# Batch 0's first weight columns by row chunks, and two up blocks begun ahead of the products with v

## Chip, cores, metric

One core of one Trainium2 chip. The metric is the device time of one execution in microseconds (us); lower is better. Five engines run their own instruction streams side by side and wait for each other by semaphores: PE (matmuls, with PEld as its weight loads), DVE (element-wise work), ACT (activations and copies), POOL (GpSimd; here it issues the loads) and SP (it issues the stores). DMA queues move the data between DRAM and the on-chip memory.

## What is computed

Attention with keys and values projected along the sequence, then a layer that takes the larger of two products:

```python
k_proj = np.einsum('ks,bhsd->bhkd', E, k)          # 64 rows instead of 1024
v_proj = np.einsum('ks,bhsd->bhkd', F, v)
attn   = softmax(q @ k_proj.T / 8)                 # 8 batches, 8 heads, 1024 x 64
x      = attn @ v_proj                             # as 8192 tokens x 512
g      = np.maximum(x @ w1, x @ w2)                # 8192 x 1024
out    = g @ w_out                                 # 8192 x 512
```

The kernel uses max(a, b) = relu(a - b) + b: it forms wd = w1 - w2 once, computes relu(x @ wd), and adds x @ (w2 @ w_out), where m = w2 @ w_out is also formed once. Inputs are float32 in DRAM; the loads convert them to float16.

## The kernel before

**Tiling.** A batch has 1024 tokens. Attention is done in four parts: two groups of four heads (g = 0, 1) times two halves of the tokens (j = 0, 1). `xt` holds x transposed: four row chunks r of 128 features (chunk r = heads 2r and 2r+1), so part (g, j) writes row chunks 2g and 2g+1 for token half j. An *up block* (j, fb) is relu(x @ wd) for token half j and 128 columns fb of wd: four matmuls, one for each row chunk r of wd and xt, summed in one PSUM bank (line 481), then a relu on ACT (line 490; for fb = 3 on DVE, line 492). Batches 1 to 7 use a form with fewer multiplications (lines 702 and 794), which begins as soon as batch 0's up blocks, m and the sums are done.

**Order.** The kernel is scheduled by hand (`manual_schedule`): every engine runs its instructions in the order in which the program issues them, and an instruction that waits holds back everything behind it on its engine. Batch 0's attention is a written-out list (lines 911 to 960); all that follows is a list `slots` of small steps, worked through in order (lines 986 to 1020 and 1126 to 1132). If a step of that list returns a function, that function runs right after the next step.

**Loads.** POOL issues every load in program order (lines 102 to 137): batch 0's k, q and v, then w2 and w1 in column pieces, w_out, then batch 1's k, v, q and batch 2's k. A weight row is addressed as (g, p, z): row chunk r = 2g + z, partition p. The first 256 columns go as four loads, w2 and w1 for g = 0 and the same for g = 1, each with both z (128 KB in float16; lines 122 to 127). Columns 256 to 511 and the rest go as one load for each z (lines 128 to 136).

**Around the change.** `step_at(g, j)` multiplies the exponentials with v (32 x 256 matmuls, line 346) into two banks and then scales them into `xt` with two DVE multiplications, o = 0 and 1 (line 401); it has a hook `between` between those two. `step_kv(.., "v")` projects v (line 189) and copies it to `vp` (line 201). `step_wd(f0, r0, r1)` forms wd for columns from f0 and row chunks r0 to r1 on DVE (line 497). `step_w2t(f0)` transposes 256 columns of w2 on PE (line 513) and copies them with ACT (line 519); this feeds m. PSUM has four banks `mm0` to `mm3` taken in turn (`mm_bank`) and a pair of double banks `att`, also in turn (`att_banks`). The order of the end of the written list, before:

```python
    step_kv(t, 4, 8, "v", True, copy=nc.scalar.copy, between=lambda: step_dn(t, 1, 1))
    step_inv(t, 1, 1)
    att_banks()
    for f0 in (0, 128):
        step_wd(f0, 0, 2, 128)
    step_at(t, 1, 0, True)
    u0, u1 = [*up_slots(t, 0)], [*up_slots(t, 1)]
    step_wd(0, 2, 4)
    step_at(t, 1, 1, True)
    first_banks = turn[0:2], turn[2:4]
    for i in range(2):
        for u in u0, u1:
            u[i](r1=2)
    step_w2t(0, True)
```

So row chunks 0 and 1 of the up blocks (0,0), (1,0), (0,1), (1,1) come after all products with v. The slots then finish (0,0) and (0,1), transpose w2's next 256 columns, finish (1,0) and (1,1), form wd for columns 256 to 511 (`wd[1]`, line 497 with all four row chunks) and go on with up block (0,2).

Of the kernel before, what the change touches and what calls it, by code (L numbers as in the profile page):

```python
# [12 lines left out]
ALU = mybir.AluOpType  # L13
# [3 lines left out]
def kernel(  # L17
# [12 lines left out]
    nc = tc.nc  # L30
# [8 lines left out]
    NDC = DM // 128  # L39
# [17 lines left out]
    turn = [0, 1, 2, 3]  # L57

    def mm_bank(dtype=FP32, n=None):
        if n is None:  # L60
            n = turn.pop(0)
            turn.append(n)
        return ps.tile([128, 512 if dtype == FP32 else 1024], dtype, tag=f"mm{n}", name="mm_ps")

    def att_banks(dtype=FP32):
        return ps.tile(
            [128, 2, 512 if dtype == FP32 else 1024], dtype, tag="att", bufs=2, name="att_ps"
        )
# [4 lines left out]
    def big(n, dtype=FP16):  # L73
        return const.tile([128, 16384 // mybir.dt.size(dtype) // 2], dtype, tag=f"big{n}", name=f"big{n}")
# [19 lines left out]
    def alloc(t, n):  # L94
        t[n] = kvq.tile([128, H, NC, D], FP16, tag="kvq", name=f"{n}_sb")

    def load_all(t, b, n, src):
        alloc(t, n)
        load(t, n, src, b, 0, H)

    def load(t, n, src, b, h0, h1):
        nc.gpsimd.dma_start(  # L102
            out=t[n][:, h0:h1],
            in_=src[b, h0:h1].rearrange("h (p c) d -> p h c d", c=NC),
        )
# [13 lines left out]
    w1_sb = big(1).rearrange("p (r f) -> p r f", r=NDC)  # L119
    w2_sb = big(2).rearrange("p (r f) -> p r f", r=NDC)  # L120
    wo_sb = const.tile([128, NFB, DM], FP16, tag="wo", name="wo_sb")
    for g in range(2):
        for w_sb, w in ((w2_sb, moe_w2), (w1_sb, moe_w1)):
            nc.gpsimd.dma_start(
                out=w_sb.rearrange("p (g z) f -> p g z f", z=2)[:, g, :, 0:256],
                in_=w.rearrange("(g p z) f -> p g z f", p=128, z=2)[:, g, :, 0:256],
            )
    for w_sb, w, f0, f1 in (
        (w2_sb, moe_w2, 256, 512), (w1_sb, moe_w1, 256, 512), (w2_sb, moe_w2, 512, DF),
# [2 lines left out]
        for z in range(2):  # L132
            nc.gpsimd.dma_start(
                out=w_sb.rearrange("p (g z) f -> p g z f", z=2)[:, :, z, f0:f1],
                in_=w.rearrange("(g p z) f -> p g z f", p=128, z=2)[:, :, z, f0:f1],
# [220 lines left out]
    def values_into(t, g, j, at_ps):  # L356
        for z in range(2):
            tiles_into(
                lambda o: at_ps[o][:, z * W : (z + 1) * W], t["ex", g, j],
                lambda rows, hh: vp_of(t, 4 * g + hh, rows, z),  # L360
            )

    def new_xt(t):
        t["xt"] = xpool.tile([128, NP2, 2, HALF], FP16, tag="xt", name="xt_sb")

    def x_out(t, g, j):
        return t["xt"][:, 2 * g : 2 * g + 2, :, j * W : (j + 1) * W]
# [16 lines left out]
    def step_inv(t, g, j):  # L384
        ld = t["ld", g, j]
        nc.scalar.activation(out=ld, in_=ld, func=ACTF.Exp, scale=-1.0)

    def step_at(t, g, j, att=False, between=None):
        if "xt" not in t:
            new_xt(t)  # L390
        ld = t.pop(("ld", g, j))
        if att:
            both = att_banks()
            at_ps = [both[:, o, :] for o in range(2)]
        else:
            at_ps = [mm_bank() for _ in range(2)]
        values_into(t, g, j, at_ps)
        for o in range(2):
            if o and between is not None:
                between()  # L400
            nc.vector.tensor_tensor(
                out=x_out(t, g, j)[:, :, o, :],
                in0=at_ps[o].rearrange("q (z n) -> q z n", z=2),
                in1=ld[:, o, None, :].broadcast_to([128, 2, W]),
                op=ALU.mult,
            )
# [61 lines left out]
    wd_sb = const.tile([128, NDC, DF], FP16)  # L468
    m_sb = const.tile([128, NDC, DM], FP16)
    w2t_sb = big(3).rearrange("p (f m) -> p f m", f=NFB)  # L470


    def up_slots(t, j):
        t["gt", j] = gt = gpool.tile([128, NFB, HALF], FP16, tag="gt", name="gt_sb")
        for fb in range(NFB):
            def up(fb=fb, r0=0, r1=NDC):
                if r0 == 0:
                    t["up", j, fb] = mm_bank(n=None if r1 == NDC else first_banks[j][fb])
                h_ps = t["up", j, fb]
                for r in range(r0, r1):  # L480
                    nc.tensor.matmul(  # L481
                        out=h_ps,
                        lhsT=wd_sb[:, r, fb * 128 : (fb + 1) * 128],
                        rhs=t["xt"][:, r, :, j * W : (j + 1) * W],
                        start=(r == 0), stop=(r == NDC - 1),
                    )
                if r1 < NDC:
                    return
                if fb != 3:
                    nc.scalar.activation(out=gt[:, fb, :], in_=h_ps, func=ACTF.Relu)  # L490
                else:
                    nc.vector.tensor_scalar_max(gt[:, fb, :], h_ps, 0.0)
            yield up


    def step_wd(f0, r0=0, r1=NDC, n=256):
        nc.vector.tensor_tensor(
            out=wd_sb[:, r0:r1, f0 : f0 + n], in0=w1_sb[:, r0:r1, f0 : f0 + n],
            in1=w2_sb[:, r0:r1, f0 : f0 + n], op=ALU.subtract,
        )  # L500

    def step_wd_rows(f0):
# [6 lines left out]
    def step_w2t(f0, att=False):  # L509
        ps_t = att_banks(FP16)[:, 0, :] if att else mm_bank(FP16)  # L510
        for f in range(2):
            for r in range(NDC):
                nc.tensor.transpose(  # L513
                    out=ps_t[:, (f * NDC + r) * 128 : (f * NDC + r + 1) * 128],
                    in_=w2_sb[:, r, f0 + f * 128 : f0 + (f + 1) * 128],
                    identity=ident16,
                )
        fb = f0 // 128
        nc.scalar.copy(
            out=w2t_sb[:, fb : fb + 2, :].rearrange("q f m -> q (f m)"), in_=ps_t  # L520
        )

# [386 lines left out]
    t = tiles[0]  # L911
# [30 lines left out]
    step_dn(t, 1, 0)  # L942
    step_sc(t, 1, 1)
    step_at(t, 0, 0)
    step_at(t, 0, 1)
    step_inv(t, 1, 0)
    step_kv(t, 4, 8, "v", True, copy=nc.scalar.copy, between=lambda: step_dn(t, 1, 1))
    step_inv(t, 1, 1)
    att_banks()
    for f0 in (0, 128):  # L950
        step_wd(f0, 0, 2, 128)
    step_at(t, 1, 0, True)
    u0, u1 = [*up_slots(t, 0)], [*up_slots(t, 1)]
    step_wd(0, 2, 4)
    step_at(t, 1, 1, True)
    first_banks = turn[0:2], turn[2:4]
    for i in range(2):
        for u in u0, u1:
            u[i](r1=2)
    step_w2t(0, True)  # L960


    load_all(tiles[1], 1, "k", k)
    wt = [lambda f0=f0: step_w2t(f0) for f0 in range(0, DF, 256)]
    wd = [lambda f0=f0: step_wd(f0) for f0 in range(0, 512, 256)]
    wd += [lambda f0=f0: step_wd_rows(f0) for f0 in range(512, DF, 256)]
    f = lambda s, *a: lambda: s(tiles[0], *a)

    def loads(b, *names):
        for n in names:  # L970
            b_ = b + (n == "k" and b < 2)
            if (b_, n) == (1, "q"):
                alloc(tiles[1], "q")
                for c in (0, NC // 2):
                    nc.gpsimd.dma_start(
                        out=tiles[1]["q"][:, :, c : c + NC // 2],
                        in_=q[1].rearrange("h (p c) d -> p h c d", c=NC)[:, :, c : c + NC // 2],
                    )
            elif (b_, n) == (2, "q"):
                alloc(tiles[2], "q")  # L980
                for h in (0, H // 2):
                    load(tiles[2], "q", q, 2, h, h + H // 2)
            elif b_ < B:
                load_all(tiles[b_], b_, n, {"k": k, "v": v, "q": q}[n])

    slots = [
        (0, lambda: u0[0](r0=2)), (1, lambda: u0[1](r0=2)), (None, lambda: loads(1, "v", "q", "k")),
        (None, lambda: step_w2t(256, True)),
        (2, lambda: u1[0](r0=2)), (3, lambda: u1[1](r0=2)),
        (None, wd[1]), (4, u0[2]), (5, u0[3]),  # L990
# [46 lines left out]
    t = tiles[1]  # L1037
    at_slot((0, 22), new_attn, t)
    at_slot((0, 22), lambda: turn.__setitem__(slice(None), [2, 3]))
    for n, x in enumerate((  # L1040
# [4 lines left out]
        for name in x.split():  # L1045
# [6 lines left out]
            else:  # L1052
                g, j = int(name[2]), int(name[3])
# [13 lines left out]
    t = tiles[2]  # L1067
# [8 lines left out]
    for b in range(3, B):  # L1076
        t = tiles[b]
        n = 2 * b - 3
# [13 lines left out]
    for i, (new, old) in enumerate(zip([*groups[1:], none], groups)):  # L1092
        n, h = divmod(i + 2, 2)
# [9 lines left out]
    for n, (b, o) in enumerate(units):  # L1103
        u = U[b, o]
# [13 lines left out]
        if n:  # L1118
            end = ("U", n - 1, 1, 6) if n > 1 else ("P", 0, 6, 1)
            m = 0 if n == last else 2  # L1120
# [45 lines left out]
```

## Time and profile before

| | |
|---|---|
| median of 3 runs | 319.96 us (319.69, 319.96, 320.4) |
| the profiled execution | 319.73 us in all, of which the profile's span is 318.0 us |
| PE busy | 312.1 us, 98% of the span, 3920 matmuls |
| PEld, DVE, ACT, POOL busy | 253.5, 240.4, 206.1, 40.0 us |
| granted TensorE clock | 1.00 in every stretch |
| HBM read and written | 57.15 MB and 16.78 MB |

A row of the timeline gives the start, the length of a run of like instructions, the engine and line, the tiles written and read, the count, and in brackets the idle time of the engine just before and what ended it. Matmuls overlap: a matmul on 512 columns is shown as 379 ns long, but eight of them in a row take 1.90 us, one every 0.216 us. DVE and ACT instructions overlap a little as well: the scaling in line 401 is shown as 0.68 us and repeats every 0.60 us. The DMA view gives the time from the start of an issue to its landing.

### The profile page before, as it was taken

What the parts mean: (1) busy time and instruction counts of PE and PEld (TensorE: products, weight loads), DVE (VectorE), ACT (ScalarE), POOL (GpSimd) and SP (SyncE); (2) the same over time, 40 slices, a digit from 0 to 9 for tenths busy, and PEclk for the clock granted to TensorE, in tenths of its full rate; (3) what the DMA queues carried; (4) which work ended last, traced back from release to release, by engine and by line L of the source; (5) the groups of instructions that cost most, each with busy time, mean ns of one, the idle gap of its engine ahead of it and who ended that gap; (6) DMA issues with size and microseconds to landing.
All of it is one profiled execution on the core that took longest, in us unless ns stands there. A gap on an engine that the chain in (4) does not pass through costs nothing.

```text
span 318.0 us, 9177 instructions
## 1 busy us (share of the span) xinstructions
PE 312.1 (98%) x3920; PEld 253.5 (80%) x3920; DVE 240.4 (76%) x437; ACT 206.1 (65%) x372; POOL 40.0 (13%) x63
## 2 busy tenths in 40 slices
PE   8989999999999999999999999999999999999996
PEld 3555588788887888788887888788887888888885
DVE  2366888877969696996969696996969696969683
ACT  2476843777776777477776778477776777765541
POOL 8269002003000300030000400040000000000000
DMA  7999999999969899899989999989969131303124
GB/s 184 203 200 197 204 206 203 207 180 157 205 119 197 152 217 245 212 182 172 237 196 213 165 200 244 221 154 179 235 142 207 45 102 35 101 33 102 35 99 132
DMA packets 76424, 53.41 MB, mean 168 GB/s; under 512 B 29536, under 2 KB 76000, under 8 KB 76384
## 3 DMA queue, kind: packets, MB, share of 16 engines
q0 software_dynamic: 30688, 28.05, 56.4%
q1 hardware_dynamic: 45408, 24.58, 32.2%
q8 instruction: 30, 0.49, 0.6%
q10 hardware_dynamic: 288, 0.20, 0.2%
q14 instruction: 10, 0.08, 0.1%
HBM read 57.15 MB, written 16.78 MB: 233 GB/s over the span
## 4 chain that ended last, share of the span: by engine, by line
PE 92%; DMA 4%; POOL 1%; ACT 1%; DVE 0%; issue 0%; POOLq 0%; DVEq 0%
PE mm_ps L794 47%; PE mm_ps L702 27%; PE mm_ps L481 4%; DMA v_sb<-in_v_dram 4%; PE att_ps L346 3%; PE mm_ps L189 3%; PE mm_ps L334 2%; PE mm_ps L590 2%; PE att_ps L231 1%; PE mm_ps L305 1%; POOL k_sb L102 0%; POOL q_sb L102 0%; ACT ld_sb L382 0%; ACT ex_sb L374 0%; DVE o_sb L892 0%; PE att_ps L513 0%
## 5 line engine op out<-in xcount | busy, mean ns | idle before, releaser
L676 ACT COPY p_sb<-mm_ps 128x512 f32<-128x512 f32 x179 | 101.8, 592 | 49.4 <-PE mm_ps L702 27.6
L794 PEld LDWEIGHTS <-big 128*128 128x128 f16 x768 | 73.6, 98 | 11.8 <-issue 3.6
L794 PE MATMUL mm_ps<-T_sb,big 128*128 128x256 f16 x576 | 76.9, 273 | 0.0
L717 DVE TENSOR_TENSOR gt_sb<-mm_ps,p_sb 128x512 f16<-128x512 f32 x56 | 38.5, 688 | 43.9 <-PE mm_ps L702 43.6
L702 PE MATMUL mm_ps<-big,big 128*128 128x256 f16 x336 | 50.4, 273 | 0.0
L702 PEld LDWEIGHTS <-big 128*128 128x128 f16 x448 | 43.8, 98 | 5.1
L794 PE MATMUL mm_ps<-wo_sb,gt_sb 128*128 128x256 f16 x256 | 42.6, 273 | 0.0
L794 PEld LDWEIGHTS <-gt_sb 128*128 128x128 f16 x376 | 35.7, 98 | 6.7 <-issue 2.7
L427 ACT ACTIVATE ex_sb<-mm_ps 128x512 f16<-128x512 f32 x50 | 27.2, 596 | 18.0 <-PE mm_ps L334 12.3
L702 PEld LDWEIGHTS <-wd_sb 128*128 128x128 f16 x336 | 32.9, 98 | 3.8
L702 PE MATMUL mm_ps<-xt_sb,wd_sb 128*128 128x256 f16 x224 | 32.8, 273 | 0.0
L456 DVE TENSOR_TENSOR xt_sb<-att_ps,ld_sb 128x1024 f16<-128x1024 f32 x26 | 31.7, 1219 | 0.2
L794 PE MATMUL mm_ps<-m_sb,xt_sb 128*128 128x256 f16 x128 | 24.4, 273 | 0.0
L824 DVE TENSOR_TENSOR o_sb<-mm_ps,p_sb 128x512 f32<-128x512 f32 x32 | 21.9, 683 | 2.8 <-ACT p_sb L853 2.0
L297 POOL COPY junk<-qt_sb 1x1 f16<-1x1 f16 x6 | 1.5, 246 | 175.1 <-DMA qt_sb<-q_sb 175.1
L720 DVE TENSOR_SCALAR gt_sb<-gt_sb 128x512 f16<-128x512 f16 (+1 forms) x60 | 21.5, 359 | 2.1
L662 DVE TENSOR_TENSOR big<-gt_sb 128x1024 f16<-128x1024 f16 x32 | 21.9, 683 | 0.0
L794 PE MATMUL mm_ps<-wo_sb,big 128*128 128x256 f16 x128 | 21.5, 273 | 0.0
L763 ACT ACTIVATE gt_sb<-mm_ps 128x512 f16<-128x512 f32 x28 | 16.8, 601 | 5.7 <-PE mm_ps L702 5.7
L794 PE MATMUL mm_ps<-T_sb,gt_sb 128*128 128x256 f16 x120 | 20.3, 273 | 0.0
L794 PEld LDWEIGHTS <-xt_sb 128*128 128x128 f16 x188 | 18.3, 98 | 2.3 <-issue 0.2
L717 DVE TENSOR_TENSOR gt_sb<-p_sb 128x512 f16<-128x512 f32 x28 | 19.1, 682 | 0.6 <-ACT p_sb L676 0.6
(113 smaller groups left out, 432.3 us busy)
## 6 DMA issues: line engine op xcount, KB each, us to landing
out_dram<-o_sb SPq DMA_DIRECT2D x62, 256.0 KB, 2.7
k_sb<-in_k_dram POOLq DMA_DIRECT2D x7, 1024.0 KB, 10.6
v_sb<-in_v_dram POOLq DMA_DIRECT2D x7, 1024.0 KB, 16.6
q_sb<-in_q_dram POOLq DMA_DIRECT2D x5, 1024.0 KB, 23.5
q_sb<-in_q_dram POOLq DMA_DIRECT2D x6, 512.0 KB, 16.2
big<-in_moe_w_dram POOLq DMA_DIRECT2D x12, 128.0 KB, 6.6
v_sb<-in_v_dram POOLq DMA_DIRECT2D x4, 256.0 KB, 13.5
wo_sb<-in_moe_w_out_dram POOLq DMA_DIRECT2D x1, 1024.0 KB, 10.8
```

Source lines behind the costliest of these rows:

```text
L189: nc.tensor.matmul(out=kv_ps[r * KP : (r + 1) * KP, h * D : (h + nh) * D], lhsT=eft[i][:, c, :], rhs=t[w][:, h0 + h : h0 + h + nh, c, :], ...
L427: nc.scalar.activation(out=t["ex", g, j][:, e, :], in_=banks[e], func=ACTF.Exp, scale=scale)
L456: nc.vector.tensor_tensor(out=x_out(t, g, j).rearrange("q z o n -> q o z n"), in0=at_ps.rearrange("q o (z n) -> q o z n", z=2), in1=ld[:, ...
L481: nc.tensor.matmul(out=h_ps, lhsT=wd_sb[:, r, fb * 128 : (fb + 1) * 128], rhs=t["xt"][:, r, :, j * W : (j + 1) * W], start=(r == 0), stop= ...
L662: nc.vector.tensor_tensor(out=S(i), in0=S(0) if x is None else x, in1=y(), op=op)
L676: copy(out=x, in_=bank)
L702: nc.tensor.matmul(out=bank[:, m * W : (m + 1) * W], lhsT=w_[:, n_, (2 * d + m) * 128 : (2 * d + m + 1) * 128], rhs=a[:, n_, :], start=(n ...
L717: nc.vector.tensor_tensor(out=c_blk(j, c), in0=two(x), in1=two(y), op=ALU.add)
L720: nc.vector.tensor_scalar_max(ap, ap, 0.0)
L763: nc.scalar.activation(out=out, in_=in_, func=ACTF.Relu)
L794: nc.tensor.matmul(out=bank[i][:, 0:CH] if two_banks else bank[:, i * CH : (i + 1) * CH], lhsT=a(c)[:, i * 128 : (i + 1) * 128], rhs=w_(c) ...
L824: nc.vector.tensor_tensor(out=o_sb, in0=two(x), in1=two(y), op=ALU.add)
```

## The change

- The first 256 columns of w2 and w1 for g = 0 are loaded by single row chunks (z = 0, then z = 1): four loads of 64 KB in place of two of 128 KB. g = 1 stays as it was, behind them.
- wd's row chunk 0 is formed in the hook of `step_at(t, 0, 1)`, ahead of that part's second scaling; row chunk 1 is formed where chunks 0 and 1 were formed before.
- The row-chunk-0 matmuls of up blocks (0,0) and (0,1) stand ahead of the products with v of the second head group. Those of (1,0) and (1,1) stand behind both, followed by row chunk 1 of all four blocks. The banks come from the same turn as before.
- `step_w2t(0, True)` is now the first slot, and in its double-bank form the step returns its ACT copy, which therefore runs after the next slot: the copies of columns 0 to 255 and 256 to 511 stand behind the relu of up block (0,0) and of (1,0).

```diff
--- before.py
+++ after.py
@@ -119,11 +119,11 @@
     w1_sb = big(1).rearrange("p (r f) -> p r f", r=NDC)
     w2_sb = big(2).rearrange("p (r f) -> p r f", r=NDC)
     wo_sb = const.tile([128, NFB, DM], FP16, tag="wo", name="wo_sb")
-    for g in range(2):
+    for g, z0, z1 in ((0, 0, 1), (0, 1, 2), (1, 0, 2)):
         for w_sb, w in ((w2_sb, moe_w2), (w1_sb, moe_w1)):
             nc.gpsimd.dma_start(
-                out=w_sb.rearrange("p (g z) f -> p g z f", z=2)[:, g, :, 0:256],
-                in_=w.rearrange("(g p z) f -> p g z f", p=128, z=2)[:, g, :, 0:256],
+                out=w_sb.rearrange("p (g z) f -> p g z f", z=2)[:, g, z0:z1, 0:256],
+                in_=w.rearrange("(g p z) f -> p g z f", p=128, z=2)[:, g, z0:z1, 0:256],
             )
     for w_sb, w, f0, f1 in (
         (w2_sb, moe_w2, 256, 512), (w1_sb, moe_w1, 256, 512), (w2_sb, moe_w2, 512, DF),
@@ -475,7 +475,7 @@
         for fb in range(NFB):
             def up(fb=fb, r0=0, r1=NDC):
                 if r0 == 0:
-                    t["up", j, fb] = mm_bank(n=None if r1 == NDC else first_banks[j][fb])
+                    t["up", j, fb] = mm_bank()
                 h_ps = t["up", j, fb]
                 for r in range(r0, r1):
                     nc.tensor.matmul(
@@ -493,10 +493,10 @@
             yield up
 
 
-    def step_wd(f0, r0=0, r1=NDC, n=256):
+    def step_wd(f0, r0=0, r1=NDC):
         nc.vector.tensor_tensor(
-            out=wd_sb[:, r0:r1, f0 : f0 + n], in0=w1_sb[:, r0:r1, f0 : f0 + n],
-            in1=w2_sb[:, r0:r1, f0 : f0 + n], op=ALU.subtract,
+            out=wd_sb[:, r0:r1, f0 : f0 + 256], in0=w1_sb[:, r0:r1, f0 : f0 + 256],
+            in1=w2_sb[:, r0:r1, f0 : f0 + 256], op=ALU.subtract,
         )
 
     def step_wd_rows(f0):
@@ -516,9 +516,15 @@
                     identity=ident16,
                 )
         fb = f0 // 128
-        nc.scalar.copy(
-            out=w2t_sb[:, fb : fb + 2, :].rearrange("q f m -> q (f m)"), in_=ps_t
-        )
+
+        def copy():
+            nc.scalar.copy(
+                out=w2t_sb[:, fb : fb + 2, :].rearrange("q f m -> q (f m)"), in_=ps_t
+            )
+
+        if att:
+            return copy
+        copy()
 
 
 
@@ -942,22 +948,22 @@
     step_dn(t, 1, 0)
     step_sc(t, 1, 1)
     step_at(t, 0, 0)
-    step_at(t, 0, 1)
+    step_at(t, 0, 1, between=lambda: step_wd(0, 0, 1))
     step_inv(t, 1, 0)
     step_kv(t, 4, 8, "v", True, copy=nc.scalar.copy, between=lambda: step_dn(t, 1, 1))
     step_inv(t, 1, 1)
     att_banks()
-    for f0 in (0, 128):
-        step_wd(f0, 0, 2, 128)
+    step_wd(0, 1, 2)
+    u0, u1 = [*up_slots(t, 0)], [*up_slots(t, 1)]
+    for x in u0[0:2]:
+        x(r1=1)
     step_at(t, 1, 0, True)
-    u0, u1 = [*up_slots(t, 0)], [*up_slots(t, 1)]
     step_wd(0, 2, 4)
     step_at(t, 1, 1, True)
-    first_banks = turn[0:2], turn[2:4]
-    for i in range(2):
-        for u in u0, u1:
-            u[i](r1=2)
-    step_w2t(0, True)
+    for x in u1[0:2]:
+        x(r1=1)
+    for x in u0[0:2] + u1[0:2]:
+        x(r0=1, r1=2)
 
 
     load_all(tiles[1], 1, "k", k)
@@ -984,7 +990,7 @@
                 load_all(tiles[b_], b_, n, {"k": k, "v": v, "q": q}[n])
 
     slots = [
-        (0, lambda: u0[0](r0=2)), (1, lambda: u0[1](r0=2)), (None, lambda: loads(1, "v", "q", "k")),
+        (None, lambda: step_w2t(0, True)), (0, lambda: u0[0](r0=2)), (1, lambda: u0[1](r0=2)), (None, lambda: loads(1, "v", "q", "k")),
         (None, lambda: step_w2t(256, True)),
         (2, lambda: u1[0](r0=2)), (3, lambda: u1[1](r0=2)),
         (None, wd[1]), (4, u0[2]), (5, u0[3]),
```

## Prediction

> **What bounds the kernel now.** I read the page first (busy shares, chain), then the timelines of PE, DVE and POOL from 20 to 28 us, where the change lies, then the DMA issues one by one, then busy time by stretch. The page, busy shares and chain:
>
> ```profile
> PE 312.1 (98%) x3920; PEld 253.5 (80%) x3920; DVE 240.4 (76%) x437; ACT 206.1 (65%) x372; POOL 40.0 (13%) x63
> ...
> PE 92%; DMA 4%; POOL 1%; ACT 1%; DVE 0%; issue 0%; POOLq 0%; DVEq 0%
> ```
>
> PE carries the end. By stretch it is busy for 47.00 of the 47 us from 28 to 75 and 175.00 of 175 from 75 to 250, with clock 1.00. So the end moves by exactly as much as the moment at which PE starts up block (0,2), unless something late in the run gives way. The PE timeline up to there:
>
> ```profile
> 21.30 0.30 PE L346 MATMUL att_ps<-ex_sb,ones 64*32 64x256 f16 x8 [0.28 <-ACT ex_sb L374]
> 21.53 0.64 PE L189 MATMUL att_ps<-v_sb,eft 128*64 128x128 f16 x16
> 22.64 0.63 PE L346 MATMUL att_ps<-ex_sb,vp_sb 64*32 64x256 f16 x32 [0.47 <-ACT vp_sb L201]
> 23.20 1.90 PE L481 MATMUL mm_ps<-xt_sb,wd_sb 128*128 128x512 f16 x8
> 24.94 0.61 PE L513 MATMUL att_ps<-ident,big 128*128 128x128 f16 x8
> 25.38 1.03 PE L481 MATMUL mm_ps<-xt_sb,wd_sb 128*128 128x512 f16 x4
> 26.25 0.61 PE L513 MATMUL att_ps<-ident,big 128*128 128x128 f16 x8
> 26.69 4.56 PE L481 MATMUL mm_ps<-xt_sb,wd_sb 128*128 128x512 f16 x20
> ```
>
> The only real hole is before 22.64: the projection of v has streamed out by 22.0 (its row ends with 0.2 us of pipeline) and the products with v wait for the copy to `vp`. The change puts two matmuls into that hole. But the last row hides a second wait: four matmuls from 26.69 at 0.216 us would bring up block (0,2) at 27.56, and it starts at 27.63; the weight-load timeline names wd (line 497) as the releaser. DVE shows why:
>
> ```profile
> 20.36 2.48 DVE L401 TENSOR_TENSOR xt_sb<-mm_ps,ld_sb 128x512 f16<-128x512 f32 x4 [0.60 <-ACT ld_sb L382]
> 22.78 0.49 DVE L497 TENSOR_TENSOR wd_sb<-big,big 128x256 f16<-128x256 f16 x2
> 23.19 1.29 DVE L401 TENSOR_TENSOR xt_sb<-att_ps,ld_sb 128x512 f16<-128x512 f32 x2
> 24.40 0.41 DVE L497 TENSOR_TENSOR wd_sb<-big,big 128x512 f16<-128x512 f16 x1
> 24.73 1.28 DVE L401 TENSOR_TENSOR xt_sb<-att_ps,ld_sb 128x512 f16<-128x512 f32 x2
> 26.88 0.69 DVE L497 TENSOR_TENSOR wd_sb<-big,big 128x1024 f16<-128x1024 f16 x1 [0.87 <-DMA big<-in_moe_w_dram]
> ```
>
> DVE has no hole from 20.36 to 26.01; then it waits for the last of columns 256 to 511, which lands at 26.8 (the issue at 21.67 lands 5.1 us later). 26.88 + 0.69 + about 0.05 of hand-over is 27.63. So three chains meet within 0.1 us: PE's own work, DVE's, and the load queue's. **Filling a hole in the first gains at most 0.07 us** while the queue lands its bytes no sooner.
>
> **Loads.** The first-column issues:
>
> ```profile
> 7.64 0.70 POOL L124 DMA_DIRECT2D big<-in_moe_w_dram  x1
> 10.76 0.71 POOL L124 DMA_DIRECT2D big<-in_moe_w_dram  x1 [2.41 <-DMA q_sb<-in_q_dram]
> 13.30 0.70 POOL L124 DMA_DIRECT2D big<-in_moe_w_dram  x1 [1.84 <-DMA k_sb<-in_k_dram]
> 15.84 0.71 POOL L124 DMA_DIRECT2D big<-in_moe_w_dram  x1 [1.84 <-DMA q_sb<-in_q_dram]
> ```
>
> They land 14.4, 11.9, 10.1 and 8.2 us after their starts: at 22.04, 22.66, 23.4 and 24.04. That is one every 0.66 us for 128 KB whatever the issue time, so a full queue sets the landings, in order. The waits show that an issue waits for the landing of the eighth before it. The change makes two more issues, so the same weights come two places later in that rule: columns 0 to 255 of g = 1 are issued at 18.32 and 19.03 (were 13.30 and 15.84). The next ten follow from 20.32 and 21.67 on, one per 0.70 us: the last of columns 256 to 511 is issued at 23.06 (was 21.67), w_out at 28.1 (was 26.71). Bytes and their order are the same, so I keep the landings: 23.4, 24.04, 26.8, and w_out at 37.5. The cover is the queue's backlog. It is least for columns 256 to 511: 5.1 us from issue to landing before, 3.7 after. POOL also issues batch 1's k, v, q and batch 2's k about 1 us later, and these wait 15 to 26 us in the queue anyway.
>
> The first row chunk's two pieces are halves: after the last v piece (21.35) w2's lands near 21.70 and w1's at **22.04**; from the other side, w1's lands no later than the whole did, 22.66. I take 22.04 to 22.1, by the cadence, and keep 22.66 as the far end.
>
> The Trainium skill (DMA: Bandwidth & Descriptors, section on the anatomy of one SWDGE DMA) speaks against splitting: about 2.0 us fixed for each DMA besides its bytes. By it, paid in series, two more would cost some 4 us (an estimate); landings 0.66 us apart, each with 128 KB, show that here it is not paid in series, and the sum goes by the landings.
>
> **DVE and PE after.** No instruction is added on either. Step by step, with the rows' own durations:
>
> 1. DVE: the third scaling starts at 21.57, so wd's chunk 0 starts at 22.18 (landing 22.1 is just met) and is done 0.29 later, 22.47. The fourth scaling follows at 22.39, wd's chunk 1 at 22.98 (landing 22.66 is met).
> 2. PE: the two moved matmuls start at 22.53 (0.05 hand-over as at 27.63): most of the hole, 22.0 to 22.53, stays. They stream for 0.44, to 22.97.
> 3. Products with v: 0.09 more for the change from wide to 64x32 matmuls (around 59.7 the same change costs that), so they start at 23.06 instead of 22.64, **0.42 later**. They and the way back take 0.56 as before: 23.62.
> 4. PE then has six up matmuls instead of eight: 6 x 0.216 = 1.30, to 24.92; before 24.94. The gain is 0.02.
> 5. But DVE's scalings wait for the products: the first starts at 23.62 (was 23.19), then 0.61, 0.60, wd's chunks 2 and 3 at 24.82, 0.33, and the last two at 25.16 and 25.76, ending 26.44 (was 26.01).
> 6. The w2 transposes take turns in the double banks that these scalings read. The first set waits for 24.23 + 0.68 + 0.05 = 24.96; then 0.45; up blocks (0,0) and (0,1) from 25.40 to 26.27 (wd's chunks 2 and 3 are ready at 25.3). The second set, free at once before (26.25 against 26.07), now waits for 26.44 + 0.05 = 26.49: **0.22 lost**. Then 0.45 and 4 x 0.216: up block (0,2) at 27.80.
> 7. wd for (0,2) is still ready at 27.63, so PE is now the late one: **27.80 against 27.63, +0.17 us.**
>
> ACT's two moved copies (1.02 us each) cost nothing: ACT is idle for 2.47 us before 25.58. Late next is the bank of up block (1,1): its relu ends near 29.95, after the second copy, and PE wants the bank at 30.4. If that cover of some 0.4 us were gone, each 0.1 us would show in full. The copies feed m's products at 38.9, far behind. w_out's consumers had 3 us from 37.57 to 40.64.
>
> **Sum.** On the profiled execution: 319.73 + 0.17 = 319.90. The median of the runs is 0.23 above that execution, so I forecast 319.96 + 0.17 = **320.1 us**.
>
> **Rivals.**
>
> - **A, forecast:** the hole is filled late and DVE passes the delay on; 0.0 to +0.4 us, 320.0 to 320.4. For it: DVE without a hole, and the double-bank order. 0.60.
> - **B, slower, DVE held by a piece:** wd's chunk 0 stands in the middle of DVE's only full stretch, and it waits for a landing with under 0.15 us to spare. Each 0.1 us beyond 22.13 delays the fourth scaling, the moved matmuls, the products and all of steps 3 to 7. At the far end, 22.66, that is 0.60 more: +0.77, 320.7. It decides against "no change" from +0.64 on, a landing at about 22.6. For it: the whole w1 piece landed only 0.1 us ahead of its use before; against: the even cadence. 0.20.
> - **C, slower, the queue runs dry:** if 3.7 us from issue to landing is too short, columns 256 to 511 land 5.1 us after 23.06, at 28.2: +1.4, 321.4. Against: no row shows 5.1 to be a floor, since backlog explains it. 0.07.
> - **D, the other way:** the extra matmuls start nearer 22.3, the banks come free in time, and the smaller pieces bring the last landing forward. The gain is 0.07 with today's landings and perhaps 0.5 if all of them came a whole 0.66 us slot earlier: 319.5 to 319.9. Nothing in the trace moves them. 0.13.
>
> **Numbers.** A measurement of this kernel can tell about 0.2%, 0.64 us, from no change. All of A, most of D and half of B are within it. Faster by more: 0.04 (D's far end); slower by more: 0.20 (B's far end, C, and runs above the median); within: 0.76. The range takes in A and B with the spread of the three runs (0.44 above their median, 0.27 below) and D's far end, and leaves out C: 319.5 to 321.0.
>
> **What would show it.** In the changed profile: two line 481 matmuls near 22.5; the products with v near 23.06; the DVE scaling at 23.6; a wait of 0.2 us before the second set of transposes; up block (0,2) at 27.8 with no wait for wd. B would show as DVE waiting for a load before wd's chunk 0; C as the last wd of columns 256 to 511 starting after 27.3. I would be wrong if up block (0,2) starts before 27.5, or if PE gains or loses anything after 28 us.

## The result, and the profile after

The changed kernel takes **322.42 us** (median of 6 runs, 321.22 to 322.96) against 320.12 us (6 runs, 319.69 to 320.61) for the kernel before: ratio 1.0068, 95% interval 1.0048 to 1.0088. (Ratios and intervals, here and below, are formed over all runs and differ from the quotient of the two medians by up to 0.0016; single runs, of the kernel before too, lie up to 4.3 us above their median, at a granted clock of 0.989.) It is slower by 2.3 us where 320.1 was forecast, outside the range and outside what counted as no change. The profiled execution of the changed kernel is the shortest of the six (321.22 us, span 319.4 us), so its profile shows less of the loss than most of them have. A second run of the same kernel (the first experiment) has its profile near the median, 322.39 us; both are used below.

The page of the changed kernel, busy shares and chain:

```profile
PE 312.2 (98%) x3920; PEld 253.7 (79%) x3920; DVE 239.8 (75%) x437; ACT 206.0 (64%) x372; POOL 41.5 (13%) x65
...
PE 88%; DMA 7%; POOL 3%; DVE 0%; issue 0%; DVEq 0%; POOLq 0%
```

PE's work is the same (312.2 us). DMA and POOL have gone from 5% to 10% of the chain: between 21 and 33 us the chain now runs through POOL's issues and a weight load. The PE timeline there, columns as before:

```profile
21.93 0.30 PE L346 MATMUL att_ps<-ex_sb,ones 64*32 64x256 f16 x8 [0.28 <-ACT ex_sb L374]
22.16 0.64 PE L189 MATMUL att_ps<-v_sb,eft 128*64 128x128 f16 x16
23.02 0.60 PE L481 MATMUL mm_ps<-xt_sb,wd_sb 128*128 128x512 f16 x2 [0.22 <-DVE wd_sb L497]
23.55 0.63 PE L346 MATMUL att_ps<-ex_sb,vp_sb 64*32 64x256 f16 x32
24.12 1.47 PE L481 MATMUL mm_ps<-xt_sb,wd_sb 128*128 128x512 f16 x6
...
27.30 0.61 PE L513 MATMUL att_ps<-ident,big 128*128 128x128 f16 x8 [0.25 <-DVE xt_sb L401]
27.75 4.48 PE L481 MATMUL mm_ps<-xt_sb,wd_sb 128*128 128x512 f16 x20
```

This run was already 0.63 us late at its first line (21.93 against 21.30), ahead of everything that the change touches: the very first load, the first piece of k, issued at 1.24 in both, landed at 8.44 instead of 7.22, and PE's first projection of k waited for it (8.58 instead of 7.35). Runs 2 and 4 below, with the same first loads, start there at 21.39 and 21.47. From there the order of events is the forecast one: the two moved matmuls in the hole, the products with v 0.28 us later still, the wait before the second transposes. The losses that were not forecast come later. On DVE:

```profile
27.72 0.69 DVE L497 TENSOR_TENSOR wd_sb<-big,big 128x1024 f16<-128x1024 f16 x1 [0.56 <-issue]
30.54 0.69 DVE L492 TENSOR_SCALAR gt_sb<-mm_ps 128x512 f16<-128x512 f32 x1 [2.13 <-PE mm_ps L481]
32.27 0.43 DVE L505 TENSOR_TENSOR wd_sb<-big,big 128x512 f16<-128x512 f16 x1 [1.04 <-DMA big<-in_moe_w_dram]
32.99 0.42 DVE L505 TENSOR_TENSOR wd_sb<-big,big 128x512 f16<-128x512 f16 x1 [0.29 <-DMA big<-in_moe_w_dram]
```

The kernel before, at the last two of these:

```profile
30.17 0.42 DVE L505 TENSOR_TENSOR wd_sb<-big,big 128x512 f16<-128x512 f16 x1
30.77 0.43 DVE L505 TENSOR_TENSOR wd_sb<-big,big 128x512 f16<-128x512 f16 x1 [0.18 <-DMA big<-in_moe_w_dram]
```

wd of columns 256 to 511 starts at 27.72 (was 26.88; its last load lands at 27.64), and wd of columns 512 on waits twice for w1. Its two loads land at 32.18 and 32.90, against 29.99 and 30.67 before; w_out at 39.82 against 37.55. PE loses 0.30 us there and 0.2 more before the projection of batch 1's v, whose load lands at 50.67 (47.72 before). From then on PE is 1.47 us behind the kernel before, about the difference of the spans (319.4 - 318.0). Of that, 0.63 us is the late start; the loads account for about 0.5 us in this execution.

Why are the loads late? POOL's issues of the first columns:

```profile
13.72 0.53 POOL L124 DMA_DIRECT2D big<-in_moe_w_dram  x1 [1.98 <-DMA k_sb<-in_k_dram]
16.26 0.53 POOL L124 DMA_DIRECT2D big<-in_moe_w_dram  x1 [2.01 <-DMA q_sb<-in_q_dram]
17.59 0.70 POOL L124 DMA_DIRECT2D big<-in_moe_w_dram  x1 [0.81 <-DMA v_sb<-in_v_dram]
19.43 0.71 POOL L124 DMA_DIRECT2D big<-in_moe_w_dram  x1 [1.14 <-DMA v_sb<-in_v_dram]
20.20 0.70 POOL L133 DMA_DIRECT2D big<-in_moe_w_dram  x1
21.53 6.33 POOL L133 DMA_DIRECT2D big<-in_moe_w_dram  x9 [0.63 <-DMA v_sb<-in_v_dram]
```

The same end of the list in the kernel before:

```profile
18.32 1.42 POOL L133 DMA_DIRECT2D big<-in_moe_w_dram  x2 [1.77 <-DMA v_sb<-in_v_dram]
20.32 0.70 POOL L133 DMA_DIRECT2D big<-in_moe_w_dram  x1 [0.58 <-DMA v_sb<-in_v_dram]
21.67 5.06 POOL L133 DMA_DIRECT2D big<-in_moe_w_dram  x7 [0.65 <-DMA v_sb<-in_v_dram]
```

Each that waits does so for the landing of the eighth load before it, as forecast. So eight loads are in flight (issued and not yet landed in full) when v's last piece has landed and the next issue goes out, at 21.67 before and at 21.53 now: before, eight of 128 KB, **1024 KB**; now four of 64 and four of 128, **768 KB**. The queue moves 128 KB in 0.66 us, so the backlog is shorter by 2 x 0.66 = 1.32 us. From 21.53 on POOL no longer waits for anything: nine issues in 6.33 us, 0.70 us each. For a load of 128 KB that is a little slower than the queue empties, so the next loads can't make up what is missing. Two loads of 256 KB (w2's columns 512 on, issued at 23.63 and 24.31) could, by about 0.6 us each, as they do in the kernel before; here the queue has run dry by the time they count.

The bytes moved show the queue running dry. Stretches of 2 us, first the kernel before, then the changed kernel's second run; the columns are the stretch, its length, the busy time of PE, PEld, DVE, ACT and POOL, the clock, the DMA share and, last, GB/s:

```profile
24.00:26.00 2.00, 2.00 (x17) 1.13 (x15) 2.00 (x4) 0.42 (x1) 1.88 (x3) 1.00 1.43 194
26.00:28.00 2.00, 2.00 (x16) 1.04 (x15) 0.70 (x2) 2.00 (x4) 2.00 (x4) 1.00 1.22 197
28.00:30.00 2.00, 2.00 (x11) 0.88 (x9) 0.43 (x1) 1.97 (x4) 1.51 (x3) 1.00 1.43 201
```

```profile
24.00:26.00 2.00, 2.00 (x23) 1.08 (x16) 2.00 (x4) 0.00 (x0) 2.00 (x4) 1.00 1.12 139
26.00:28.00 2.00, 1.94 (x16) 0.97 (x14) 1.20 (x3) 1.49 (x3) 2.00 (x4) 1.00 0.81 84
28.00:30.00 2.00, 2.00 (x11) 0.80 (x9) 0.30 (x1) 2.00 (x5) 2.00 (x3) 1.00 1.04 156
```

2 x (194 + 197 + 201) = 1184 KB in these 6 us before, 2 x (139 + 84 + 156) = 758 KB now: 426 KB missing, about 2.1 us at 200 KB per us. PE feels it behind the place that rival C named, in columns 512 on. The second run's PE:

```profile
27.41 4.58 PE L481 MATMUL mm_ps<-xt_sb,wd_sb 128*128 128x512 f16 x20
31.83 1.06 PE L513 MATMUL mm_ps<-ident,big 128*128 128x128 f16 x16
34.48 7.20 PE L481 MATMUL mm_ps<-xt_sb,wd_sb 128*128 128x512 f16 x32 [1.60 <-DVE wd_sb L505]
```

Before, the last two rows are:

```profile
31.09 1.06 PE L513 MATMUL mm_ps<-ident,big 128*128 128x128 f16 x16
31.98 7.07 PE L481 MATMUL mm_ps<-xt_sb,wd_sb 128*128 128x512 f16 x32
```

The run is 0.74 us behind at the first (0.48 of it a late start as above: 21.78 against 21.30, with the first piece of k at 8.29) and 2.50 at the second: 1.76 us are lost in one wait for wd, that is for w1's columns 512 on, landing at 33.9 and 34.2.

### The profile page after: what moved, and what is told of

It is laid out like the page before. It is cut to its first block, busy times and chain, and to the rows that moved or that the text cites. A ratio compares the mean times of both kernels' runs of the same rounds, so it can differ in the third digit from the quotient of the medians.

```text
span 319.4 us, 9180 instructions
## 1 busy us (share of the span) xinstructions
PE 312.2 (98%) x3920; PEld 253.7 (79%) x3920; DVE 239.8 (75%) x437; ACT 206.0 (64%) x372; POOL 41.5 (13%) x65
## 4 chain that ended last, share of the span: by engine, by line
PE 88%; DMA 7%; POOL 3%; DVE 0%; issue 0%; DVEq 0%; POOLq 0%
PE mm_ps L800 47%; PE mm_ps L708 27%; DMA v_sb<-in_v_dram 4%; PE att_ps L346 3%; PE mm_ps L189 3%; PE mm_ps L334 2%; DMA big<-in_moe_w_dram 2%; PE mm_ps L481 2%; PE mm_ps L596 2%; POOL big L133 1%; PE att_ps L231 1%; POOL v_sb L102 1%; PE mm_ps L305 1%; POOL k_sb L102 0%; POOL q_sb L102 0%
## 5 line engine op out<-in xcount | busy, mean ns | idle before, releaser
L297 POOL COPY junk<-qt_sb 1x1 f16<-1x1 f16 x6 | 2.4, 404 | 173.8 <-DMA qt_sb<-q_sb 173.8
L800 PE MATMUL mm_ps<-wo_sb,big 128*128 128x256 f16 x128 | 21.5, 273 | 0.0
```

Source lines behind the costliest of these rows:

```text
L800: nc.tensor.matmul(out=bank[i][:, 0:CH] if two_banks else bank[:, i * CH : (i + 1) * CH], lhsT=a(c)[:, i * 128 : (i + 1) * 128], rhs=w_(c) ...
```

## The experiments

Three theories. **Q**: the queue runs dry, because two of the eight loads in flight are small (rival C of the prediction, in its closer form). **O**: the new order costs the time. **P**: the split pieces, or added issues as such, upset the queue whatever stands behind them. Times are medians; "before" is the kernel before, timed beside the run on the same chip.

**1. The changed kernel again** (no edit).

> The changed kernel once more, for a second profile and a closer time. Theory Q (the two added issues on POOL let the load queue run dry, so the later weights, w_out and batch 1's v land late and PE waits for them) expects +1.5 to +2.6 us on the kernel before, PE waits at the up blocks of columns 512 and above or at batch 1's projection of v, and w_out landing 1 us or more later than 37.5. Theory O (the new order: DVE and the double banks delay PE before 28 us) expects the same total, but nearly all of it gained before up block (0,2), at 29 us or later, and no PE wait for a load after that.

Measured: 322.28 us against 320.37, ratio 1.0048 (1.0021 to 1.0074). The loss is repeatable; its profile is shown above.

**2. The four loads alone, in the order of before.** The edit is the first hunk of the diff.

> The kernel before with the four single-row-chunk loads alone; its order of work is untouched. Theory Q expects most of the loss: +1.2 to +2.4 us, with the same PE waits after 32 us. Theory O expects 0.0 to +0.3 us.

Measured: 322.75 us, ratio 1.0058 (1.0030 to 1.0085). The loads alone cost as much as the whole change. 129, 98 and 134 GB/s from 24 to 30 us; PE:

```profile
28.20 3.63 PE L481 MATMUL mm_ps<-xt_sb,wd_sb 128*128 128x512 f16 x16 [0.40 <-DVE wd_sb L497]
31.66 0.22 PE L513 MATMUL mm_ps<-ident,big 128*128 128x128 f16 x1
32.89 1.01 PE L513 MATMUL mm_ps<-ident,big 128*128 128x128 f16 x15 [1.01 <-DMA big<-in_moe_w_dram]
34.89 3.33 PE L481 MATMUL mm_ps<-xt_sb,wd_sb 128*128 128x512 f16 x14 [0.98 <-DVE wd_sb L505]
```

Three waits, all for weight loads, two of them by way of wd: columns 256 to 511, then w2 and w1 from 512 on. Theory O falls as the main cause.

**3. The new order alone, with the loads of before.** All hunks but the first.

> The changed kernel with the loads of the kernel before (each of w2 and w1 of the first columns with both row chunks of g = 0 in one load). Theory Q expects 0.0 to +0.9 us: the forecast's +0.2, and up to 0.6 more because wd's first chunk now waits for the whole w1 piece at about 22.7. Theory O expects +1.5 to +2.4 us.

Measured: 321.03 us, ratio 1.0033 (1.0002 to 1.0065). The queue holds (196, 196, 177 GB/s). What is lost is lost early, on DVE and then on PE:

```profile
22.87 0.29 DVE L497 TENSOR_TENSOR wd_sb<-big,big 128x256 f16<-128x256 f16 x1 [0.52 <-DMA big<-in_moe_w_dram]
```

```profile
23.22 0.60 PE L481 MATMUL mm_ps<-xt_sb,wd_sb 128*128 128x512 f16 x2 [0.94 <-DVE wd_sb L497]
```

wd's chunk 0 waits for the whole w1 piece, and the moved matmuls with it. That is rival B at its far end, here because the piece is not split; the profiled run is 0.94 us above the profiled run of before and the median 0.66 above, where B's far end was priced at 0.77.

**4. Fewer issues later on.** The change, with w1's columns 512 to 1023 as one load for each z, which brings the number of weight issues back to that of before.

```diff
-        (w1_sb, moe_w1, 512, 768), (w1_sb, moe_w1, 768, DF),
+        (w1_sb, moe_w1, 512, DF),
```

> The changed kernel with w1's columns 512 to 767 and 768 to 1023 as one load for each z, so that the number of weight issues is the 14 of the kernel before. Theory Q expects the loss to shrink to 0.0 to +0.9 us, with w_out landing near 38. Theory O expects no change from the changed kernel, +1.5 to +2.6 us.

Measured: 323.85 us, ratio 1.0103 (1.0066 to 1.0139), the worst of all. Theory Q's number missed. The profile shows where the time goes:

```profile
29.91 3.63 PE L481 MATMUL mm_ps<-xt_sb,wd_sb 128*128 128x512 f16 x16 [1.71 <-DVE wd_sb L497]
33.38 1.06 PE L513 MATMUL mm_ps<-ident,big 128*128 128x128 f16 x16
34.67 0.39 PE L481 MATMUL mm_ps<-xt_sb,wd_sb 128*128 128x512 f16 x1 [0.23 <-DVE wd_sb L505]
36.18 2.12 PE L481 MATMUL mm_ps<-xt_sb,wd_sb 128*128 128x512 f16 x9 [1.12 <-DVE wd_sb L505]
```

The queue is dry by 24 to 26 us (134 GB/s), and the merged loads are issued from 25.31 on: larger loads behind the hole don't fill it. And a load lands as a whole, so the first half of w1's columns came only at 34.09 and 35.60 (33.91 and 34.17 in run 1). So the total number of issues is not the point; the bytes in flight at 21.5 may be. The next runs were made for that.

**5. Two small loads that nobody reads.** Before, with two loads of 128 x 4 elements between the first columns of g = 0 and g = 1, and nothing else.

```diff
+    tiny = const.tile([128, 2, 4], FP16, tag="tiny", name="tiny_sb")
     for g in range(2):
+        for i in range(2 * g):
+            nc.gpsimd.dma_start(out=tiny[:, i], in_=moe_w_out[0:128, 4 * i : 4 * i + 4])
```

> The kernel before with two loads of 4 columns of w_out to 128 rows (1 KB of float16 each, read by nobody) put between the first-column loads of g = 0 and g = 1. Theory Q in its closer form (at most eight loads are in flight, so two small ones among them take 256 KB out of the backlog, and the queue runs dry at about 24 us) expects +1.4 to +2.6 us and a dip of the bytes moved from about 190 to below 150 KB per us between 24 and 29 us. Rival P (it is the split pieces of the weights, not the count of loads, that upset the queue) expects 0.0 to +0.4 us and no dip.

Measured: 322.14 us against 320.03, ratio 1.0062 (1.0043 to 1.0081). Two loads of 1 KB, which move nothing to speak of, cost the whole 2.1 us, by the same waits:

```profile
33.10 1.01 PE L516 MATMUL mm_ps<-ident,big 128*128 128x128 f16 x15 [1.05 <-DMA big<-in_moe_w_dram]
```

No weight is split here, so it is not the pieces themselves. Two slots of the eight hold next to nothing, six hold 768 KB, the same as in the change.

**6. One such load** (`range(g)` in place of `range(2 * g)`).

> The same with one such load. Theory Q expects 128 KB less in flight, which leaves a cover of about 2.9 us where 3.6 us stood before and some 2.1 us is the floor: 0.0 to +0.5 us, no dip or a slight one. If every added issue costs the same, +0.7 to +1.3 us. Rival P expects 0.0 to +0.2 us.

Measured: 320.08 us, ratio 1.0011 (0.9986 to 1.0036): nothing that can be measured. There is a slack of one slot, and it is nearly used up: 193, 174, 144 GB/s.

**7. The change with only w1's first piece split**, w2's whole: one issue more than before instead of two.

> The changed kernel with only w1's first columns of g = 0 split; w2's stay one load, so one issue is added instead of two. wd's first chunk can start when w1's first piece lands, at about 22.4. Theory Q expects no dry queue and thus the cost of the new order alone, +0.1 to +0.7 us. Rival P expects about half of the loss or more, +0.9 to +1.6 us.

Measured: 320.36 us, ratio 1.0005 (0.9994 to 1.0015). PE:

```profile
22.15 0.30 PE L349 MATMUL att_ps<-ex_sb,ones 64*32 64x256 f16 x8 [0.28 <-ACT ex_sb L377]
...
23.36 0.60 PE L484 MATMUL mm_ps<-xt_sb,wd_sb 128*128 128x512 f16 x2 [0.34 <-DVE wd_sb L500]
23.89 0.63 PE L349 MATMUL att_ps<-ex_sb,vp_sb 64*32 64x256 f16 x32
```

No later row of PE up to 38 us waits for a load. (This profiled run was 0.85 us late at 22.15, before the change acts; its time is 320.87.) The bytes moved dip here too (187, 174, 150 GB/s), but PE pays nothing for it. The new order does what the prediction worked out for it, and is worth nothing.

**8. The two later ACT copies alone, in the kernel before.**

> The kernel before with the two ACT copies of the transposed w2 moved behind the next relu, alone. All theories expect no difference, -0.3 to +0.3 us, since ACT is idle before them and their readers come later.

Measured: 320.05 us, ratio 0.9996 (0.9985 to 1.0007). The copies cost nothing, as forecast.

**9. The split, with the bytes put back.** The order of before; g = 0 split as in the change, but g = 1 is loaded 512 columns wide, and columns 256 to 511 of g = 0 follow: loads 9 to 16 are 4 x 64, 2 x 256 and 2 x 128 KB, 1024 KB.

```diff
+    for g, z0, z1, f1 in ((0, 0, 1, 256), (0, 1, 2, 256), (1, 0, 2, 512)):
         for w_sb, w in ((w2_sb, moe_w2), (w1_sb, moe_w1)):
...
+    for w_sb, w in ((w2_sb, moe_w2), (w1_sb, moe_w1)):
+        nc.gpsimd.dma_start(
+            out=w_sb.rearrange("p (g z) f -> p g z f", z=2)[:, 0, :, 256:512],
...
-        (w2_sb, moe_w2, 256, 512), (w1_sb, moe_w1, 256, 512), (w2_sb, moe_w2, 512, DF),
+        (w2_sb, moe_w2, 512, DF),
```

> The order of work is that of before. The loads of g = 0 are split as in the change (four of 64 KB), but w2 and w1 of g = 1 then come as 512 columns (256 KB each), and columns 256 to 511 of g = 0 follow as one load of 128 KB each: eight issues with 1024 KB, as many bytes in flight behind v's last piece as before. Theory Q (with two of the eight loads in flight made small, too few bytes stand in the queue when v ends, and it runs dry near 24 us): the bytes are back, so the queue stays at 190 to 200 GB/s from 24 to 30 us and w_out ends near 37.6. w1's 256 KB for g = 1 end near 25.3 instead of 24.0, so wd's chunks 2 and 3 and the second halves of the first up blocks come later: +0.3 to +1.0 us in all, and PE loses nothing to loads after 28 us. Theory P (small pieces themselves upset the queue, whatever stands behind them): the hole between 25 and 29 us is there as in the loads alone, 100 to 140 GB/s, and the time is +1.8 to +2.5.

Measured: 320.70 us against 319.97, ratio 1.0018 (1.0008 to 1.0027). The same 64 KB pieces, and no hole:

```profile
24.00:26.00 2.00, 1.77 (x15) 1.01 (x14) 1.18 (x4) 0.30 (x1) 2.00 (x4) 1.00 1.35 194
26.00:28.00 2.00, 1.75 (x14) 0.88 (x14) 1.64 (x3) 1.87 (x4) 2.00 (x3) 1.00 1.23 192
28.00:30.00 2.00, 2.00 (x11) 0.88 (x9) 0.00 (x0) 2.00 (x4) 1.54 (x3) 1.00 1.36 181
```

What is left is the expected price of the wide load, paid where it was expected, at wd's chunks 2 and 3 (w1 for g = 1 lands at 25.33):

```profile
25.42 0.42 DVE L502 TENSOR_TENSOR wd_sb<-big,big 128x512 f16<-128x512 f16 x1 [0.82 <-DMA big<-in_moe_w_dram]
```

**10. The whole change with these loads.**

> The whole change, with the loads of the run before: g = 0 split, g = 1 512 columns wide. Theory Q: no hole after 24 us, PE waits for wd's chunks 2 and 3 (near 25.3 + 0.4) and for nothing from 28 us on: +0.3 to +1.0 us on before, so below the change by about 1 us. Theory P: the hole stays, +1.5 to +2.5 us. If the order itself were worth anything with the queue full, this run would lie below the loads alone with the same pieces.

Measured: 320.80 us, ratio 1.0028 (1.0013 to 1.0044); 191, 188, 186 GB/s. More than half of the change's loss (2.3 us, 1.9 in run 1) is gone, with nothing altered but the loads; the order adds 0.1 us to run 9.

**11. Run 5's two loads in a later place**, behind w_out.

> Before, with the two unread loads of 128 x 4 placed behind w_out instead of behind the first two weight loads: the same number of added issues, at a place where a load of 1024 KB is in flight. Theory Q: nothing, within 0.2 us of before. If added issues cost as such (POOL's time, or a fixed time for each load in the queue): +1 to +2 us as in the run with the two loads in the early place.

Measured: 320.14 us, ratio 1.0001 (0.9992 to 1.0009). The same two issues cost nothing where a load of 1024 KB stands in flight before them. Theory P falls in both forms: the pieces by runs 5 and 9, added issues as such by runs 6 and 11. (Run 9 has the 14 weight issues of the kernel before, so it says nothing of added issues. That the eight slots hold fewer bytes and that the weights behind them are issued later are two sides of one thing here; no run parts them.)

All kernels together. The first column is the shortest time from the start of an issue to the start of its data, over loads 13 to 19, worked out from the trace as the landing of the median one of the 16 engines, less 0.66 us for each 128 KB, less the start of the issue:

| kernel | us from issue to data, least | mean GB/s, 24 to 30 us | w_out landed | ratio to before |
|---|---|---|---|---|
| before | 3.56 | 197 | 37.55 | 1 |
| 10, the change, bytes put back | 3.30 | 188 | 38.08 | 1.0028 |
| 11, two small, late | 3.29 | 195 | 37.95 | 1.0001 |
| 3, the order alone | 3.24 | 189 | 37.89 | 1.0033 |
| 9, split, bytes put back | 3.21 | 189 | 37.92 | 1.0018 |
| 8, the copies alone | 3.14 | 190 | 38.07 | 0.9996 |
| 7, one piece split | 2.81 | 170 | 38.96 | 1.0005 |
| 6, one small | 2.69 | 170 | 38.12 | 1.0011 |
| the change | 2.34 | 151 | 39.82 | 1.0068 |
| 2, the loads alone | 2.18 | 120 | 41.06 | 1.0058 |
| 4, merged later | 2.14 | 127 | 40.67 | 1.0103 |
| 5, two small | 2.11 | 121 | 40.84 | 1.0062 |
| 1, the change again | 2.06 | 126 | 40.42 | 1.0048 |

Nothing came below about 2.1 us; I take that for what an issue needs to its first data when nothing stands ahead of it, and what is above it for backlog. This is argued from the table and not shown by a run of its own, but the packets agree within 0.3 us: the first packet of w2's columns 512 on starts 2.67 to 2.94 us after its issue in the kernel before and in runs 3, 8 and 11, and 1.86 to 2.24 us after it in the seven kernels from 7 down. Before, the backlog at its least was 3.56 - 2.1, about 1.5 us. Two small slots take 1.3 us of it. None of the runs points to a version faster than the kernel before: with the queue full, the new order gains nothing (7, 10).

**What stays open.** The hole is longer than the missing backlog. In run 1 load 19 (256 KB), issued at 24.04, is at 4.48 us by the table's measure, though the queue was nearly empty and its first packet starts at 26.28, 2.24 us after the issue; its 16 engines land between 27.86 and 30.51, where before the same load's are within 1.05 us (27.03 to 28.07). Some of that is lost inside packets: from 24 to 30 us a packet of 1 KB takes 0.10 us in the median in both, but five in run 1 take 0.5 to 1.73 us, and none before takes over 0.38. Why a queue that has run dry starts again so unevenly, and why the loss differs from run to run (321.22 to 322.96), no run here tells.

## Why the prediction was wrong

- **The step that failed** is in the part on loads: "Bytes and their order are the same, so I keep the landings: 23.4, 24.04, 26.8, and w_out at 37.5", with "the cover is the queue's backlog ... 5.1 us before, 3.7 after". The issue times were near (g = 1 forecast at 18.32 and 19.03, measured 17.59 and 19.43; the last of columns 256 to 511 forecast at 23.06, measured 22.92; w_out 28.1 and 27.82). Two things were not asked. First, how much of the 3.7 us a load needs for itself: about 2.1 us to its first data, 0.66 us of transfer, and 0.7 us or more until the slowest engine has landed, 3.5 us in all, so that hardly any of the 3.7 was backlog. Second, whether POOL can rebuild the backlog in time: at 0.70 us an issue against 0.66 us a transfer it can't with loads of 128 KB. In place of the 3.7 us that load took 4.72 (4.20 in run 1) from issue to landing. Landings: 26.8 forecast and 27.64 measured (27.53 in run 1); w_out 37.5 and 39.82 (40.42).
- **Rival C** was the right mechanism; the prediction gave it a chance of 0.07 and left it out of the range. Its sign came true (the last wd of columns 256 to 511 at 27.72 and 27.61, after 27.3). Its price, +1.4 us for that one load, was in the wrong place: those columns cost PE 0.1 us at most in the changed kernel. The hole grew behind them and PE paid at columns 512 on: 0.30 us in one run, 1.76 in the other. "Against: no row shows 5.1 to be a floor" was true and no answer: the floor is lower, and the change reached it.
- **"If PE gains or loses anything after 28 us"** was named as a sign of being wrong, and was it.
- **Steps 1 to 4, right.** From its own late start (0.63 us), the changed kernel has wd's chunk 0 at 22.68 (22.18 + 0.63 = 22.81 forecast), the moved matmuls at 23.02 (23.16), the products at 23.55 (23.69).
- **Steps 5 to 7, right.** The second transposes wait 0.22 us in runs 3 and 7, the 0.22 worked out. In the profiled run of the change they wait 0.42: wd's chunks 2 and 3 came 0.2 us late there, since w1's load for g = 1 has its slowest engine at 25.44 (median 23.19). The order's cost, 0.17 us forecast, is +0.33 us in the medians of run 7 and 0.1 between runs 9 and 10, below what can be measured.
- **Copies at nothing, right** (run 8). **Rival B** did not come: the split w1 piece had landed by 21.91 and DVE's own order set chunk 0. Run 3 shows what it would have been without the split. (Its far end is mis-summed, by its own figures: from 22.13 to 22.66 are 0.53 us and not 0.60, so +0.70 and not +0.77.) **Rival D** did not come: the smaller pieces brought nothing forward later on.
- The Trainium skill (DMA: Bandwidth & Descriptors, section on the anatomy of one SWDGE DMA) gives about 2.0 us fixed for each DMA. The prediction set this aside since landings 0.66 us apart show that it is not paid in series, and that holds. But the runs show a time for each load of its own, 2.06 to 2.34 us from issue to data in the dry runs, which is hidden only as long as other loads stand in front: it should have been weighed as a floor under the cover. It is near the page's figure but not the same span: the page puts most of its 2.0 us behind the last byte, on the confirmation of the write, while the time here lies ahead of the data and takes in POOL's 0.70 us for the issue.

## What to carry to other kernels

Where a fixed number of loads may be in flight, a small load takes a whole slot: count the bytes in flight, not the issues, and look at the moment when the issuing engine stops waiting for landings. Compare the least time from issue to data with its floor; once the issuing engine needs longer for an issue (0.70 us) than the queue for its bytes (0.66 us), lost backlog is not rebuilt by loads of that size. Work that is moved into a hole of the critical engine should be tried with its loads left alone, and the loads alone, since here the second cost 2.4 us (run 2) and the first 0.7 (run 3).

## What the runs showed of the hardware

- A load's landing is that of its slowest engine: before, the last of the 16 comes 0.75 to 1.4 us after the median one on loads 13 to 22; in run 4 the last of columns 256 to 511 had its median engine at 26.65 and its slowest at 29.09, and PE waited for the latter.
- Two loads of 1 KB among eight cost 2.1 us (run 5), one costs nothing (run 6), and two in another place cost nothing (run 11). In the queue itself such a load takes 0.19 us.
- PE was already 0.48 to 0.85 us late at 21.3 us in three profiled runs (the change, 1 and 7) and 0.3 us late at most in the ten others. In those three the first load of all, 256 KB of k, landed at 8.29 to 8.61 us, in the others at 7.08 to 7.64, and no change touches it. How often the executions without a trace have this, and how much of the change's loss is such a late start, nothing here tells; run 2, whose profile has hardly any (0.09 us), loses 2.4 us to the loads alone.
